# Cluster similarities of an attention kernel: the token tile becomes the stationary operand, the centroids move

## The chip, the cores and the metric

The kernel runs on one core of a Trainium2 chip. Its engines are TensorE (PE, its weight loads PEld), VectorE (DVE), ScalarE (ACT), GpSimd (POOL) and SyncE (SP), which only issues DMAs here. Each takes its instructions in its own order and waits for the others by semaphores. The metric is the device time of one execution in microseconds, median of the runs; lower is better.

## The reference, cut to what matters

Attention over 2 x 8 heads of 768 tokens and 64 dimensions, in which a token attends only to tokens of its own cluster; two dense layers follow (token count 1536, model width 512).

```python
q_n = q / (np.linalg.norm(q, axis=-1, keepdims=True) + 1e-06)      # k_n, c_n alike
q_assign = np.argmax(np.einsum('bhsd,hcd->bhsc', q_n, c_n), axis=-1)   # 16 centroids a head
k_assign = np.argmax(np.einsum('bhsd,hcd->bhsc', k_n, c_n), axis=-1)
mask = q_assign[:, :, :, None] == k_assign[:, :, None, :]
scores = np.where(mask, scale * np.matmul(q, k.transpose(0, 1, 3, 2)), -1000000000.0)
attn = softmax(scores)            # max subtracted, 1e-9 added to the sum
out = np.matmul(attn, v)
# then: h = (x @ w1) * (x @ w2) @ w3 @ w_out; out = softplus(h @ w_in) @ w_out2
```

The part at hand is the two `einsum` lines: for each token of q and of k its product with the 16 centroids of its head.

## The kernel before, in words

Work goes by pairs of heads (8 pairs). For each pair there is a *preparation* and then 12 *slots* of attention, six a head. The instructions of each engine stand in the order in which the program writes them: a loop over slots calls, for each slot, what two tables (`PE` and `EV`, for pairs 2 to 7) or (`PE1` and `EV1`, for pair 1) name for it; pair 0 is prepared by straight code ahead of the loop. A table's key is a slot relative to 12 times the pair's number, so pair 3's entry -11 is done in slot 25. Within a slot the order is: product for the row minimum (`mx_pe`, L629) and its minimum on VectorE (L638), the preparation steps, four score matmuls (`st_pe`, L659) with an exponential on ScalarE (L666), the products with v (`av_pe`, L674), and, woven in, steps of a product of two weight matrices (L520, L539).

Preparation of a pair before the change:

- `t1_pe`/`t1_ev`: q and k of one head lie side by side (64 + 64) and are transposed on TensorE, then written as two float32r tiles of 128 x 768 whose sum is the exact value: `H` (ScalarE, L318) and `L` (VectorE, L319). Rows 0 to 63 are q (scaled by -1/8), rows 64 to 127 are k.
- `centroid_turn` (once): the normalised centroids of all heads, transposed, are written into `cst`, one 128 x 128 tile a head: for the q rows and the k rows a high and a low part in columns of their own, the rest zero.
- `sims_pe` (L371): the head's `cst` tile is stationary, `H` and then `L` move, both heads of the pair summed into one PSUM bank, in two groups of tokens (512 and 256 columns): 8 matmuls. The outcome has centroids on partitions and tokens in columns.
- `sims_ev` (L61, ScalarE): the two groups are copied to `sT` in SBUF.
- `simsT_pe` (L391): for each of six chunks of 128 tokens `sT` is stationary and a 128 x 64 matrix `halves` moves. This turns tokens to partitions and adds high and low part.
- `assign` (VectorE, L404 to L418): times the reciprocal norm, maximum over 16 centroids, first hit, one-hot. `back_pe` (L428) and `back_ev` (L440) turn the one-hot rows back, and DMAs (L446) bring them into the q and k tiles of the scores.

The norms come on another way (GpSimd or ScalarE squares, VectorE sums, ScalarE roots, L282 and L283) and are first needed by `assign`. Three PSUM banks (`rb`) go round between all these steps by `take` and `give`. After the 96 slots come the dense layers (L848, L870, L1073, L1142), bound by matmuls alone.

Of the kernel before, what the change touches and what calls it, by code (L numbers as in the profile page):

```python
# [8 lines left out]
F32 = mybir.dt.float32  # L9
F32R = mybir.dt.float32r  # L10
# [3 lines left out]
ALU = mybir.AluOpType  # L14
# [4 lines left out]
P = 128  # L19
# [3 lines left out]
def f32(ap):  # L23
    return ap.bitcast(F32)
# [3 lines left out]
def fused_kernel(ctx: ExitStack, tc, q, k, v, centroids, w1, w2, w3, wo, w_in, w_o2, out):  # L28
# [6 lines left out]
    nc = tc.nc  # L35
    B, H, S, D = q.shape
# [94 lines left out]
    nc.vector.memset(bigcol[:64], BIG)  # L131
    nc.vector.memset(bigcol[64:], 1.0)

    halves = cpool.tile([P, 4, NCL], F32, name="halves")
    iv = identF.rearrange("p (g t b) -> p g t b", t=2, b=NCL)
    nc.vector.tensor_tensor(out=halves, in0=iv[:, :, 0], in1=iv[:, :, 1], op=ALU.add)
    qkcol = cpool.tile([P, 1], F32, name="qkcol")
    nc.vector.memset(qkcol[:64], -0.125)
    nc.vector.memset(qkcol[64:], 1.0)
# [40 lines left out]
    apT = pool(es_prep, "apT", bufs=4)  # L180


    cst = ap1.tile([P, H, P], F32R, name="cst")
    nc.gpsimd.memset(f32(cst), 0.0)
    oh = ap1.tile([P, QC, P], BF16, name="oh")
    nc.gpsimd.memset(oh, 0.0)
# [45 lines left out]
    def centroid_turn():  # L232
        cn = PR["cn"]
        m = take()
        nc.tensor.transpose(m[:, :P], cn.rearrange("p t d -> p (t d)"), identF)

        for ni, sc in enumerate((-8.0, 1.0)):
            rows = slice(64 * ni, 64 * ni + 64)
            mv = m[rows, :P].rearrange("p (g j c) -> p g j c", j=2, c=NCL)
            cv = cst[rows].rearrange("p (g j) x -> p g j x", j=2)  # L240
            for j in range(2):
                o = 64 * ni + 32 * j
                hi, lo = cv[:, :, j, o : o + NCL], cv[:, :, j, o + NCL : o + 2 * NCL]
                nc.vector.tensor_scalar(
                    out=hi, in0=mv[:, :, j, :], scalar1=sc, scalar2=None, op0=ALU.mult
                )
                nc.vector.scalar_tensor_tensor(
                    out=lo, in0=mv[:, :, j, :], scalar=sc, in1=f32(hi),
                    op0=ALU.mult, op1=ALU.subtract,
                )  # L250
        give(m)

    def norm_sq(pi, j):
# [103 lines left out]
        nc.gpsimd.tensor_copy(KT[0][D : D + 32, 0, :], a[D : D + 32])  # L357
        nc.gpsimd.tensor_copy(QT[0][D : D + 32, 0, :], l[:32])

    SG = ((0, 512), (512, S))  # L360

    def sims_pe(pi, g):
        if g == 0:
            PR["sT"] = ring.tile([P, S], F32, tag="w3k", name=f"sT{pi}")
        h0 = (2 * pi) % H
        m = take()
        c0, c1 = SG[g]
        n = 0
        for j in range(2):
            for t in (PR["H", j], PR["L", j]):  # L370
                nc.tensor.matmul(  # L371
                    m[:, : c1 - c0], cst[:, h0 + j, :], t[:, c0:c1],
                    start=(n == 0), stop=(n == 3),
                )
                n += 1
        PR["sm", g] = m

    def sims_ev(pi, g):
        c0, c1 = SG[g]
        act_copy(PR["sT"][:, c0:c1], PR["sm", g][:, : c1 - c0])  # L380
        give(PR["sm", g])

    NG = 4
    NA = NG * QC

    NS = NA * NCL

    def simsT_pe(pi):
        PR["sx"] = take()
        for c in range(QC):  # L390
            nc.tensor.matmul(  # L391
                PR["sx"][:, c * NG * NCL : (c + 1) * NG * NCL],
                PR["sT"][:, c * P : (c + 1) * P], halves.rearrange("p g b -> p (g b)"),
                start=True, stop=True,
            )

    def assign(pi, i):

# [188 lines left out]
    def load_v(pi):  # L587
# [10 lines left out]


    PE = {  # L600
        -16: [(t1_pe, 0)], -15: [(t1_pe, 1)], -14: [(t1_pe, 2)], -13: [(t1_pe, 3)], -11: [(sims_pe, 0)],
        -10: [(sims_pe, 1)], -9: [(simsT_pe,)], -5: [(back_pe,)],
    }
    EV = {
        -24: [(load_qk,)], -20: [(norm_sq, 0)], -19: [(norm_fold, 0)],
        -18: [(norm_sq, 1), (norm_sum, 0)], -17: [(norm_fold, 1)],
        -16: [(t1_ev, 0)], -15: [(t1_ev, 1), (norm_sum, 1), (norm_root,)],
        -14: [(t1_ev, 2), (norm_rec, 0)], -13: [(t1_ev, 3), (norm_rec, 1)], -11: [(sims_ev, 0), (norm_rec, 2)],
        -10: [(sims_ev, 1)], -8: [(assign, 0), (t_dma, 0)], -7: [(assign, 1)],
        -5: [(back_ev,)], -4: [(m_dma, 0), (t_dma, 1), (m_dma, 1)], 1: [(load_v,)],  # L610
    }

# [126 lines left out]
    class Feed:  # L739
# [39 lines left out]
        def take(self, n=1):  # L779
            now = [self.fly.pop(0) for _ in range(min(n, len(self.fly)))]  # L780
            tiles = []
            for t, (pl, store, key) in now:
                hi, lo = (
                    pl().tile([P, 512], F32R, tag="w", name=f"w{x}{key[0]}_{key[1]}") for x in "hl"
                )
                tiles.append((hi, lo))
                store[key] = (hi, lo)
            apart = decp is not None
            ds = decode([
                (t, decp.tile([P, 512], F32, tag="dec", name=f"d{k[0]}_{k[1]}") if apart else None)  # L790
                for t, (_, _, k) in now
            ])
            if apart:
                self.load(len(now))
            for (hi, lo), d in zip(tiles, ds):
                act_copy(hi, d)
                pool_sub(lo, d, f32(hi))
            if not apart:
                self.load(len(now))
# [86 lines left out]
    def steps(tab, s):  # L886
# [5 lines left out]


    PE1 = {
        0: [(t1_pe, 0)], 1: [(t1_pe, 1)], 2: [(t1_pe, 2)], 3: [(t1_pe, 3)], 4: [(sims_pe, 0)],
        5: [(sims_pe, 1)], 6: [(simsT_pe,)], 9: [(back_pe,)],
    }
    EV1 = {
        0: [(t1_ev, 0), (norm_sq, 0)], 1: [(t1_ev, 1), (norm_sum, 0)], 2: [(t1_ev, 2), (norm_sq, 1), (t_dma, 0)],
        3: [(t1_ev, 3), (norm_sum, 1), (norm_root,)], 4: [(sims_ev, 0), (norm_rec, 0), (norm_rec, 1)],  # L900
        5: [(sims_ev, 1), (norm_rec, 2), (t_dma, 1)], 7: [(assign, 0)], 8: [(assign, 1)],
        9: [(back_ev,)], 10: [(m_dma, 0), (m_dma, 1)],
    }

# [6 lines left out]
    with tc.manual_schedule():  # L911
        act_dma = nc.scalar.dma_start
        load_qk(0, [0])
        centroid_load()
        load_qk(0, [1], act_dma)
        nc.scalar.preload_act_table_set("natural_log_exp_and_others")
        w_load()
        w_load()
        t1_pe(0, 0)
        t1_pe(0, 1)  # L920
        centroid_prep()
        t1_ev(0, 0)
        t1_ev(0, 1)
        t1_pe(0, 2)
        t1_pe(0, 3)
        t1_ev(0, 2)
        t1_ev(0, 3)
        centroid_turn()
        norm_sq(0, 0)
        norm_sq(0, 1)  # L930
        load_qk(1)
        t_first()
        sims_pe(0, 0)
        sims_pe(0, 1)
        sims_ev(0, 0)
        sims_ev(0, 1)
        norm_sum(0, 0)
        norm_sum(0, 1)
        simsT_pe(0)
        norm_root(0)  # L940
        for n in range(W0):
            w_step(n, WALL[:1])
        norm_rec(0, 0)
        norm_rec(0, 1)
        norm_rec(0, 2)
        t_dma(0, 1)
        t_dma(0, 0)
        assign(0, 0)
        assign(0, 1)
        back_pe(0)  # L950
        back_ev(0)
        m_dma(0, 1, act_dma)
        w_load()
        load_v(0)
        for n in range(W0):
            w_step(n, WALL[1:])
        for s in range(NSLOT + ML + AL):
            j = s - ML
            a = j - AL
            if s < NSLOT:  # L960
                mx_pe(s)
                mx_red(s)
            if s and s % QC == 0 and s <= NSLOT:
                m_row(s // QC - 1)
            weights = s >= ML
            if weights:
                w_step(wk[0], "hlpqe")
            if a > 0 and a % 3 == 0:
                av_ev(a // 3 - 1)
            for tab in (PE1, EV1):  # L970
                for f, *x in tab.get(s, ()):
                    f(1, *x)
            if s == 4:
                load_qk(2)
            if s == 8:
                load_v(1)
            steps(PE, s)
            steps(EV, s)
            if 0 <= j < NSLOT:
                st_pe(j)  # L980
                st_exp(j)
            if weights:
                w_step(wk[0], "Abcds")
            if 0 <= a:
                av_pe(a)
            if weights:
                w_step(wk[0], "Tm")
                wk[0] += 1

            for g in range(NH):  # L990
                r = s - (ML + AL + QC * g + QC - 1)
                if r in (2, 4, 6):
                    r_ev(g, r // 2 - 1)
                if r == 8:
                    x_norm(2 * g)
                    x_norm(2 * g + 1)
            if wk[0] == NWSTEP:
                feed.load(3)

            if wk[0] > NWSTEP and s >= WSLOT:  # L1000
                i, k = divmod(s - WSLOT, 4)
                if i < 2:
                    feed.part(0, k)
                    if k == 3:
                        feed.take(1)
                        taken += 1
                elif i < 5:
                    feed.part(i - 2, k)
# [202 lines left out]
```

## Time and profile before

| | |
|---|---|
| device time, three runs | 849.31, 851.35, 854.03 us (median 851.35) |
| span of the profiled execution | 846.2 us |
| its own time beside the span | not listed; the runs shown lie 3.1 to 7.8 us above the span |
| TensorE busy | 798.1 us, 94% of the span, 3553 records |
| VectorE, ScalarE, GpSimd busy | 497.7, 396.5, 245.8 us |
| attention with preparation | about the first 375 us |

The span runs from the first to the last instruction of one profiled execution; the device time also has what lies around it. Busy TensorE time is modelled at the ends of matmuls, so the distance of starts says more on its pace than a duration does. A group "x12" in a view ordered by time is a run of like instructions, and its time is from the first start to the last end; in the chain that ended last a piece is the time by which it carried the end.

### The profile page before, as it was taken

The page shows a single profiled execution, that of the slowest core. Times are in us where ns is not written, and L with a number is a line of the kernel's source. Part 1 is how long each engine was busy: PE and PEld are TensorE (multiplying, and loading weights), DVE is VectorE, ACT ScalarE, POOL GpSimd, SP SyncE. Part 2 cuts the span into 40 slices and gives each one's busy share as a digit, 9 for nine tenths or more (in the row PEclk, how much of TensorE's full clock was granted, in tenths as well). Part 3 has the DMA queues.
Part 4 walks back from the last instruction along what each step waited for, and adds up shares of the span by engine and source line. Part 5 has one row for each costly group of instructions (what it writes and reads, how often), then busy time and mean ns, then how long its engine had stood idle before and what let it go on. Part 6 is the DMA issues. An engine that isn't in the chain of part 4 may idle for free.

```text
span 846.2 us, 10075 instructions
## 1 busy us (share of the span) xinstructions
PE 798.1 (94%) x3553; PEld 635.7 (75%) x3553; DVE 497.7 (59%) x826; ACT 396.5 (47%) x683; POOL 245.8 (29%) x232
## 2 busy tenths in 40 slices
PE   3589999979999998999999999999999999999997
PEld 3467777857777775778888888887877788888886
DVE  5878565576866565528532445564998644454443
ACT  3355445455443554555433245445555644454443
POOL 4145141145132121135201122321444222222220
PEclk9789999998999999999999999999999999999999
DMA  6875755655552555035311133430210100001001
GB/s 164 201 165 160 169 141 134 149 146 138 151 120 67 138 137 124 12 93 184 107 44 50 50 99 101 149 100 1 74 50 1 50 1 1 1 2 48 1 0 51
DMA packets 77491, 75.61 MB, mean 89 GB/s; under 512 B 46336, under 2 KB 62848, under 8 KB 77440
## 3 DMA queue, kind: packets, MB, share of 16 engines
q1 hardware_dynamic: 75476, 73.84, 32.7%
q10 hardware_dynamic: 1964, 1.12, 0.5%
q8 instruction: 28, 0.46, 0.2%
q14 instruction: 23, 0.19, 0.1%
HBM read 50.41 MB, written 3.24 MB: 63 GB/s over the span
## 4 chain that ended last, share of the span: by engine, by line
PE 77%; DVE 13%; DMA 3%; SPq 2%; ACT 2%; issue 2%; POOL 1%; DVEq 0%; POOLq 0%; ACTq 0%
PE avb L674 11%; PE rb L848 8%; PE sb L848 8%; PE sb L1073 6%; PE sb L659 6%; PE rb L1073 6%; PE mb L1142 6%; PE rb L539 5%; PE mb L870 4%; PE mb L629 3%; PE rb L1142 3%; PE avb L1142 3%; PE avb L870 2%; PE rb L870 2%; DVE mn L638 2%
## 5 line engine op out<-in xcount | busy, mean ns | idle before, releaser
L674 PE MATMUL avb<-E,v 128*128 128x384 f32 x384 | 143.3, 496 | 0.4 <-ACT t L61 0.4
L638 DVE TENSOR_REDUCE mn<-mb 128x1 f32<-128x768 f32 x92 | 87.7, 953 | 90.1 <-PE mb L629 89.5
L66 POOL TENSOR_TENSOR u<-u,t 128x512 f32<-128x512 f32 x47 | 66.7, 1420 | 167.3 <-DVE u L1096 167.3
L666 ACT ACTIVATE E<-sb 128x768 f32<-128x768 f32 x96 | 77.6, 808 | 74.3 <-PE sb L659 73.4
L659 PE MATMUL sb<-q,k 128*128 128x384 f32 (+1 forms) x384 | 92.7, 364 | 4.6 <-ACT E L666 4.0
L674 PEld LDWEIGHTS avb<-E,v 128*128 128x128 f32 x384 | 72.6, 194 | 28.8 <-ACT t L61 2.1
L629 PE MATMUL mb<-k,q 128*128 128x384 f32 x184 | 65.6, 438 | 11.6 <-DVE mn L638 9.1
L659 PEld LDWEIGHTS sb<-q,k 128*128 128x128 f32 (+1 forms) x384 | 67.8, 196 | 10.1 <-ACT E L666 6.8
L1073 PE MATMUL sb<-ys,wh_i 128*128 128x512 f32 x192 | 64.2, 395 | 3.5 <-ACT t L1084 2.2
L1073 PE MATMUL rb<-ys,wh_i 128*128 128x512 f32 x192 | 63.4, 392 | 0.0
L848 PE MATMUL rb<-xs,wh 128*128 128x512 f32 x192 | 61.7, 392 | 0.0
L848 PE MATMUL sb<-xs,wh 128*128 128x512 f32 x192 | 61.6, 392 | 0.0
L1086 DVE TENSOR_SCALAR u<-t 128x512 f32<-128x512 f32 x48 | 21.1, 440 | 68.1 <-ACT t L1085 68.1
L629 PEld LDWEIGHTS mb<-k,q 128*128 128x128 f32 x184 | 33.8, 196 | 30.9 <-DVE mn L638 13.2
L66 POOL TENSOR_TENSOR wl_o<-d_o,wh_o 128x512 fp32r<-128x512 f32 x16 | 21.6, 1351 | 121.3 <-ACT wh_o L61 121.3
L721 POOL TENSOR_TENSOR xT<-t,R 64x384 f32<-64x384 f32 x32 | 34.0, 1083 | 59.5 <-DMA R<-rd 59.3
L69 DVE TENSOR_TENSOR gl<-u,gh 128x512 fp32r<-128x512 f32 x48 | 39.6, 825 | 18.6 <-ACT gh L61 17.8
L1095 ACT ACTIVATE u<-u 128x512 f32<-128x512 f32 x48 | 30.4, 633 | 35.7 <-DVE t L1092 35.6
L1073 PEld LDWEIGHTS sb<-ys,wh_i 128*128 128x128 f32 x192 | 35.9, 188 | 13.6 <-ACT t L1084 3.3
L1073 PEld LDWEIGHTS rb<-ys,wh_i 128*128 128x128 f32 x192 | 36.1, 188 | 8.0
L848 PEld LDWEIGHTS rb<-xs,wh 128*128 128x128 f32 x192 | 36.1, 188 | 7.9
L848 PEld LDWEIGHTS sb<-xs,wh 128*128 128x128 f32 x192 | 36.1, 188 | 7.8
(208 smaller groups left out, 1787.1 us busy)
## 6 DMA issues: line engine op xcount, KB each, us to landing
w3r<-in_moe_w_dram SPq DMA_DIRECT2D x16, 512.0 KB
w12r<-in_moe_w_dram SPq DMA_DIRECT2D x16, 512.0 KB
wir<-in_moe_w_in_dram SPq DMA_DIRECT2D x16, 512.0 KB
wor<-in_moe_w_out_dram SPq DMA_DIRECT2D x16, 512.0 KB
q<-H SPq DMA_DIRECT2D x15, 384.0 KB
w3r<-in_moe_w_out_dram SPq DMA_DIRECT2D x8, 512.0 KB
k<-L SPq DMA_DIRECT2D x16, 192.0 KB
v<-in_v_dram SPq DMA_DIRECT2D x16, 192.0 KB
```

Source lines behind the costliest of these rows:

```text
L66: nc.gpsimd.tensor_tensor(out=o, in0=i, in1=hi, op=ALU.subtract)
L69: return nc.vector.tensor_tensor(out=o, in0=i, in1=hi, op=ALU.subtract)
L539: nc.tensor.matmul(m, a[:, ks], bb, start=(mc == 0 and x == 0), stop=(mc == NK - 1 and x == 2))
L629: nc.tensor.matmul(bank[:, hf, :HALF], QT[g][:, 0, c * P : (c + 1) * P], KT[g][:, 0, hf * HALF : (hf + 1) * HALF], start=True, stop=True,)
L638: nc.vector.tensor_reduce(out=MN[g][:, c : c + 1], in_=mx_bank(s)[:, :, :HALF], op=ALU.min, axis=AX.XY)
L659: nc.tensor.matmul(sbank[:, i, :HALF], KT[g][: P - 31 * n, n, ks], QT[g][: P - 31 * n, n, qs], start=(n == 0), stop=(n == 1),)
L666: nc.scalar.activation(E[j], sbank[:, :, :HALF], AF.Exp, scale=-1.0)
L674: nc.tensor.matmul(avbank[:, :HALF], V[g][:, 2 * kp + i, :], e[:, i, :], start=(kp == 0 and i == 0), stop=(kp == 2 and i == 1),)
L848: nc.tensor.matmul(bk[:, :BLK], a[:, sl], bb, start=(n == 0), stop=(n == 3 * CC - 1))
L870: nc.tensor.matmul(ybank[e][:, :BLK], a[:, es], bb, start=(fc == 0 and n == 0), stop=(fc == NFC - 1 and n == 2),)
L1073: nc.tensor.matmul(hbank[(bl * NF2 + fc) % 4][:, :BLK], a[:, sl], bb, start=(n == 0), stop=(n == 3 * CC - 1))
L1142: nc.tensor.matmul(ob, a[:, sl], bb, start=(fc == 0 and n == 0), stop=(fc == NF2 - 1 and n == 2),)
```

## The change

The similarities come out with tokens on partitions at once: the 128-token chunk of `H` or `L` is the stationary operand and the centroids move, 32 columns at a time (16 for q, 16 for k). For each head and chunk three products are summed in PSUM: H with the high part of the centroids, H with the low part, L with the high part. (The fourth, L with the low part, was in the sum before and is left out.) `cst` is laid out by high and low part, q and k rows, head and centroid; its high part is written by ScalarE, its low part by VectorE. `sT`, `halves`, `sims_ev`, `simsT_pe` and two uses of a PSUM bank a pair are gone. In the tables the similarities stand in slots -10 and -9, one head each, instead of -11 and -10 with the product with `halves` in -9.

```diff
--- before.py
+++ after.py
@@ -131,9 +131,6 @@
     nc.vector.memset(bigcol[:64], BIG)
     nc.vector.memset(bigcol[64:], 1.0)
 
-    halves = cpool.tile([P, 4, NCL], F32, name="halves")
-    iv = identF.rearrange("p (g t b) -> p g t b", t=2, b=NCL)
-    nc.vector.tensor_tensor(out=halves, in0=iv[:, :, 0], in1=iv[:, :, 1], op=ALU.add)
     qkcol = cpool.tile([P, 1], F32, name="qkcol")
     nc.vector.memset(qkcol[:64], -0.125)
     nc.vector.memset(qkcol[64:], 1.0)
@@ -180,7 +177,7 @@
     apT = pool(es_prep, "apT", bufs=4)
 
 
-    cst = ap1.tile([P, H, P], F32R, name="cst")
+    cst = ap1.tile([P, 2, 2, H, NCL], F32R, name="cst")
     nc.gpsimd.memset(f32(cst), 0.0)
     oh = ap1.tile([P, QC, P], BF16, name="oh")
     nc.gpsimd.memset(oh, 0.0)
@@ -236,18 +233,12 @@
 
         for ni, sc in enumerate((-8.0, 1.0)):
             rows = slice(64 * ni, 64 * ni + 64)
-            mv = m[rows, :P].rearrange("p (g j c) -> p g j c", j=2, c=NCL)
-            cv = cst[rows].rearrange("p (g j) x -> p g j x", j=2)
-            for j in range(2):
-                o = 64 * ni + 32 * j
-                hi, lo = cv[:, :, j, o : o + NCL], cv[:, :, j, o + NCL : o + 2 * NCL]
-                nc.vector.tensor_scalar(
-                    out=hi, in0=mv[:, :, j, :], scalar1=sc, scalar2=None, op0=ALU.mult
-                )
-                nc.vector.scalar_tensor_tensor(
-                    out=lo, in0=mv[:, :, j, :], scalar=sc, in1=f32(hi),
-                    op0=ALU.mult, op1=ALU.subtract,
-                )
+            mv = m[rows, :P].rearrange("p (h b) -> p h b", b=NCL)
+            hi, lo = cst[rows, 0, ni], cst[rows, 1, ni]
+            act_copy(hi, mv, scale=sc)
+            nc.vector.scalar_tensor_tensor(
+                out=lo, in0=mv, scalar=sc, in1=f32(hi), op0=ALU.mult, op1=ALU.subtract
+            )
         give(m)
 
     def norm_sq(pi, j):
@@ -357,42 +348,22 @@
         nc.gpsimd.tensor_copy(KT[0][D : D + 32, 0, :], a[D : D + 32])
         nc.gpsimd.tensor_copy(QT[0][D : D + 32, 0, :], l[:32])
 
-    SG = ((0, 512), (512, S))
-
-    def sims_pe(pi, g):
-        if g == 0:
-            PR["sT"] = ring.tile([P, S], F32, tag="w3k", name=f"sT{pi}")
-        h0 = (2 * pi) % H
-        m = take()
-        c0, c1 = SG[g]
-        n = 0
-        for j in range(2):
-            for t in (PR["H", j], PR["L", j]):
-                nc.tensor.matmul(
-                    m[:, : c1 - c0], cst[:, h0 + j, :], t[:, c0:c1],
-                    start=(n == 0), stop=(n == 3),
-                )
-                n += 1
-        PR["sm", g] = m
-
-    def sims_ev(pi, g):
-        c0, c1 = SG[g]
-        act_copy(PR["sT"][:, c0:c1], PR["sm", g][:, : c1 - c0])
-        give(PR["sm", g])
-
     NG = 4
     NA = NG * QC
 
     NS = NA * NCL
 
-    def simsT_pe(pi):
-        PR["sx"] = take()
+    def sims_pe(pi, j):
+        if j == 0:
+            PR["sx"] = take()
+        h = 2 * pi % H + j
+        sx = PR["sx"][:, :NS].rearrange("p (c n j b) -> p c j n b", n=2, j=2, b=NCL)
         for c in range(QC):
-            nc.tensor.matmul(
-                PR["sx"][:, c * NG * NCL : (c + 1) * NG * NCL],
-                PR["sT"][:, c * P : (c + 1) * P], halves.rearrange("p g b -> p (g b)"),
-                start=True, stop=True,
-            )
+            cs = slice(c * P, (c + 1) * P)
+            for i, (x, w) in enumerate((("H", 0), ("H", 1), ("L", 0))):
+                nc.tensor.matmul(
+                    sx[:, c, j], PR[x, j][:, cs], cst[:, w, :, h], start=(i == 0), stop=(i == 2)
+                )
 
     def assign(pi, i):
 
@@ -598,15 +569,15 @@
 
 
     PE = {
-        -16: [(t1_pe, 0)], -15: [(t1_pe, 1)], -14: [(t1_pe, 2)], -13: [(t1_pe, 3)], -11: [(sims_pe, 0)],
-        -10: [(sims_pe, 1)], -9: [(simsT_pe,)], -5: [(back_pe,)],
+        -16: [(t1_pe, 0)], -15: [(t1_pe, 1)], -14: [(t1_pe, 2)], -13: [(t1_pe, 3)],
+        -10: [(sims_pe, 0)], -9: [(sims_pe, 1)], -5: [(back_pe,)],
     }
     EV = {
         -24: [(load_qk,)], -20: [(norm_sq, 0)], -19: [(norm_fold, 0)],
         -18: [(norm_sq, 1), (norm_sum, 0)], -17: [(norm_fold, 1)],
         -16: [(t1_ev, 0)], -15: [(t1_ev, 1), (norm_sum, 1), (norm_root,)],
-        -14: [(t1_ev, 2), (norm_rec, 0)], -13: [(t1_ev, 3), (norm_rec, 1)], -11: [(sims_ev, 0), (norm_rec, 2)],
-        -10: [(sims_ev, 1)], -8: [(assign, 0), (t_dma, 0)], -7: [(assign, 1)],
+        -14: [(t1_ev, 2), (norm_rec, 0)], -13: [(t1_ev, 3), (norm_rec, 1)], -11: [(norm_rec, 2)],
+        -8: [(assign, 0), (t_dma, 0)], -7: [(assign, 1)],
         -5: [(back_ev,)], -4: [(m_dma, 0), (t_dma, 1), (m_dma, 1)], 1: [(load_v,)],
     }
 
@@ -892,13 +863,13 @@
 
 
     PE1 = {
-        0: [(t1_pe, 0)], 1: [(t1_pe, 1)], 2: [(t1_pe, 2)], 3: [(t1_pe, 3)], 4: [(sims_pe, 0)],
-        5: [(sims_pe, 1)], 6: [(simsT_pe,)], 9: [(back_pe,)],
+        0: [(t1_pe, 0)], 1: [(t1_pe, 1)], 2: [(t1_pe, 2)], 3: [(t1_pe, 3)],
+        5: [(sims_pe, 0)], 6: [(sims_pe, 1)], 9: [(back_pe,)],
     }
     EV1 = {
         0: [(t1_ev, 0), (norm_sq, 0)], 1: [(t1_ev, 1), (norm_sum, 0)], 2: [(t1_ev, 2), (norm_sq, 1), (t_dma, 0)],
-        3: [(t1_ev, 3), (norm_sum, 1), (norm_root,)], 4: [(sims_ev, 0), (norm_rec, 0), (norm_rec, 1)],
-        5: [(sims_ev, 1), (norm_rec, 2), (t_dma, 1)], 7: [(assign, 0)], 8: [(assign, 1)],
+        3: [(t1_ev, 3), (norm_sum, 1), (norm_root,)], 4: [(norm_rec, 0), (norm_rec, 1)],
+        5: [(norm_rec, 2), (t_dma, 1)], 7: [(assign, 0)], 8: [(assign, 1)],
         9: [(back_ev,)], 10: [(m_dma, 0), (m_dma, 1)],
     }
 
@@ -932,11 +903,8 @@
         t_first()
         sims_pe(0, 0)
         sims_pe(0, 1)
-        sims_ev(0, 0)
-        sims_ev(0, 1)
         norm_sum(0, 0)
         norm_sum(0, 1)
-        simsT_pe(0)
         norm_root(0)
         for n in range(W0):
             w_step(n, WALL[:1])
```

TensorE in slots 13 to 15, where pair 2 is prepared, before the change: `H`, `L` and `cst` as above, `sb` the scores, `avb` the products with v, `mb` the products for the row minimum, `rb` the shared banks.

```order
L371 MATMUL rb_102<-L_1_478,cst 128x512
L659 MATMUL sb<-q_212,k_213 128x384 x4
L674 MATMUL avb<-E_536,v_0_285 128x384 x2
L629 MATMUL mb<-k_335,q_334 128x384 x2
L371 MATMUL rb_100<-H_0_431,cst 128x256
L371 MATMUL rb_100<-L_0_432,cst 128x256
L371 MATMUL rb_100<-H_1_477,cst 128x256
L371 MATMUL rb_100<-L_1_478,cst 128x256
L659 MATMUL sb<-q_212,k_213 128x384 x4
L674 MATMUL avb<-E_565,v_0_285 128x384 x2
L629 MATMUL mb<-k_335,q_334 128x384 x2
L391 MATMUL rb_101<-halves,sT_553 128x64 x6
```

And TensorE after the change in slots 14 and 15, from the last chunk of the first head to the first chunk of the second:

```order
L364 MATMUL rb_99<-cst,H_0_463 128x2x16 x2
L364 MATMUL rb_99<-cst,L_0_464 128x2x16
L630 MATMUL sb<-q_206,k_207 128x384 x4
L645 MATMUL avb<-E_591,v_0_298 128x384 x2
L600 MATMUL mb<-k_348,q_347 128x384 x2
L364 MATMUL rb_99<-cst,H_1_509 128x2x16 x2
L364 MATMUL rb_99<-cst,L_1_510 128x2x16
```

What moved: the blocks of 4, 4 and 6 matmuls in three slots became two blocks of 18 in two slots, in the slots of the second block and of the `halves` product; the steps around them are the same.

ScalarE at pair 0, ahead of the loop, before the change (`q` and `k` are the tiles of the scores, `nrm` the norms):

```order
L318 ACTIVATE H_1_182<-rb_100,qkcol 128x384
L61 ACTIVATE q_212<-H_0_158 64x768
L61 ACTIVATE k_213<-H_0_158 64x768
L61 ACTIVATE sT_219<-rb_102 128x512
L61 ACTIVATE sT_219<-rb_100 128x256
L282 ACTIVATE nrm_230<-nrm_230 128x24
L283 ACTIVATE nrm_230<-nrm_230 128x24
```

And after it:

```order
L309 ACTIVATE H_1_180<-rb_98,qkcol 128x384
L63 ACTIVATE cst<-rb_99 64x128 x2
L61 ACTIVATE q_206<-H_0_156 64x768
L61 ACTIVATE k_207<-H_0_156 64x768
L273 ACTIVATE nrm_249<-nrm_249 128x24
L274 ACTIVATE nrm_249<-nrm_249 128x24
```

What moved: the two `sT` copies that stood ahead of the norms are gone, and two writes of `cst` stand ahead of the copies to `q` and `k`. On VectorE at this place eight writes of `cst` (64 elements each) became two (128 each).

## Rows read from the trace of the kernel before

**Rows 1.** The page's busy time of each engine: us, share, instructions.

```profile
PE 798.1 (94%) x3553; PEld 635.7 (75%) x3553; DVE 497.7 (59%) x826; ACT 396.5 (47%) x683; POOL 245.8 (29%) x232
```

**Rows 2.** The page's chain that ended last: share of the span by engine.

```profile
PE 77%; DVE 13%; DMA 3%; SPq 2%; ACT 2%; issue 2%; POOL 1%; DVEq 0%; POOLq 0%; ACTq 0%
```

**Rows 3.** Stretches: length, busy (count) of PE, PEld, DVE, ACT, POOL, clock, DMA.

```profile
170.00:200.00 30.00, 25.38 (x107) 18.64 (x106) 20.63 (x34) 15.62 (x29) 15.45 (x16) 0.89 0.55 140
200.00:320.00 120.00, 118.21 (x571) 92.78 (x570) 78.95 (x137) 56.95 (x95) 31.72 (x37) 1.00 0.52 127
```

**Rows 4.** The chain by time at the start: start us, us, piece.

```profile
14.07 0.22 DVE cst L247
...
15.32 2.91 PE rb L371 x8
...
18.66 0.23 ACT nrm L282
...
21.44 0.58 DVE rb L404
...
39.77 1.29 PE rb L391 x12
...
42.37 0.57 DVE rb L404
```

**Rows 5.** The same chain around pair 3's similarities, 100 to 112 us.

```profile
103.11 0.93 PE rb L371 x4
...
106.84 0.48 PE rb L371 x4
107.32 0.70 PE sb L659 x4
...
109.67 1.28 PE rb L391 x12
110.95 0.76 PE sb L659 x4
```

**Rows 6.** Groups by line, first 320 us: busy us, mean ns, idle before.

```profile
L629 PE MATMUL mb<-k,q 128*128 128x384 f32 x160 | 55.8, 430 | 8.3 <-DVE mn L638 5.7 <-ACT k L436 2.0 <-DMA k<-sg 0.6
...
L629 PEld LDWEIGHTS mb<-k,q 128*128 128x128 f32 x160 | 29.2, 196 | 23.7 <-DVE mn L638 9.2 <-issue 2.5 <-DVE w3r L493 1.2
...
L539 PEld LDWEIGHTS rb<-woh,w3th 128*128 128x128 f32 x64 | 12.1, 189 | 5.0 <-DVE w3tl L69 0.9
...
L391 PEld LDWEIGHTS rb<-halves,sT 128*128 128x128 f32 x96 | 12.0, 196 | 0.1
...
L428 PEld LDWEIGHTS <-oh 128*128 128x128 bf16 x48 | 3.1, 108 | 7.8 <-issue 6.4 <-DVE oh L418 1.4
```

**Rows 7.** TensorE in order of time, 55 to 85 us: start us, us, group.

```profile
66.06 1.45 PE L391 MATMUL rb<-halves,sT 128*128 128x64 f32 x12
...
79.17 0.51 PE L428 MATMUL rb<-identB,oh 128*128 128x128 bf16 x6
79.48 0.95 PE L659 MATMUL sb<-q,k 128*128 128x384 f32 x4
```

**Rows 8.** TensorE's waits, 55 to 320 us: total us, times, longest.

```profile
PE sb L659 <- ACT E L666: 4.0, 3, 2.8
```

**Rows 9.** Instructions in order of time, first 40 us.

```profile
18.05 1.84 PE L391 MATMUL rb<-halves,sT 128*128 128x64 f32 x12
```

**Rows 10.** Stretches of the start, columns as in rows 3.

```profile
25.00:30.00 5.00, 2.83 (x13) 2.46 (x14) 3.76 (x7) 2.68 (x3) 0.00 (x0) 0.50 0.58 172
...
40.00:45.00 5.00, 2.49 (x17) 1.75 (x16) 4.70 (x9) 0.65 (x2) 1.66 (x3) 1.00 1.07 217
```

**Rows 11.** Instructions in order of time around 188 us; idle before in brackets.

```profile
188.64 0.58 ACT L318 ACTIVATE H<-rb,qkcol 128x384 fp32r<-128x384 f32 x1 [3.77 <-DMA k<-H]
...
189.97 1.65 PE L659 MATMUL sb<-q,k 128*128 128x384 f32 x4 [2.82 <-ACT E L666]
```

## The prediction

> **What bounds the kernel.** I read the shares by engine first, then the chain that ended last, then the stages, then the few microseconds around one pair's similarities. TensorE is busy 798.1 of 846.2 us [rows 1], and 77% of the chain that ended last is TensorE, 2% ScalarE [rows 2]. From 200 to 320 us TensorE works 118.21 of 120 us, ScalarE 56.95 [rows 3]. So in most of the attention stage anything that lengthens TensorE's own stream lengthens the kernel, and anything taken off ScalarE does not shorten it. Two stretches differ. Between 170 and 200 us TensorE stands idle 4.6 us (25.38 of 30 busy) [rows 3]; and the start runs along the preparation of the first two pairs, through VectorE and ScalarE too [rows 4].
>
> The change touches eight pairs of heads. Pairs 2 to 7 are prepared inside the attention stage, at places where TensorE is the bound; pairs 0 and 1 at the start.
>
> **What goes out of TensorE's stream.** For one pair of the full stream (pair 3) the chain holds three blocks: four matmuls of 512 columns, 0.93 us; four of 256, 0.48 us; and the product with `halves`, 12 records, 1.28 us [rows 5]. Together 2.69 us a pair. The six matmuls with `halves` appear as twelve records; both their operands are plain float32.
>
> **What comes in.** Now 36 matmuls a pair: two heads, six chunks of 128 tokens, three terms, each with a 128x128 stationary tile and 32 moving columns. No matmul of this kind is in the trace, so I bound it.
> - The nearest row is the product with `halves`: a 128x128 stationary tile and few moving columns (64). Its records follow each other at 1.28 / 12 = 0.107 us [rows 5], although one load alone takes 196 ns [rows 6]: loads overlap matmuls and each other, and the load sets the pace. A float32r load is as long as a float32 load, 189 against 196 ns [rows 6]. So 36 x 0.107 = 3.85 us.
> - The narrowest float32r row is the 256-column one: 0.48 / 4 = 0.120 us a matmul [rows 5], so 36 x 0.120 = 4.32 us.
> - The row below is the bfloat16 transpose: six loads and six matmuls of 128 columns stand between 79.17 and 79.48 us, 0.052 us for a load and its matmul [rows 7], so 36 x 0.052 = 1.87 us.
> - The end above is the way of the `halves` product: if a narrow matmul made two records like it, 72 x 0.107 = 7.70 us.
>
> I take 0.107, the row with nearly the same shape. H is moved against by two centroid tiles in turn, so one stationary tile serves two matmuls; L629 is such a place too, and has 160 loads for 160 matmuls [rows 6], so no load is saved.
>
> At 0.107 a pair costs 3.85 - 2.69 = 1.16 us more. Six pairs: +7.0 us. The score matmuls behind the load-paced block take 0.76 us instead of 0.70 [rows 5]; there are now two such blocks a pair instead of one, about +0.05 x 6 = +0.3 us.
>
> The trace has bfloat16 loads at 108 ns on the mean against 189 for float32r [rows 6]: the quick kind of load is not given to float32r here. The Trainium skill (TensorE: Matmul & The Clock Gate, section "Weight-path perf modes — Fast Weight Load (FWL) and DoubleRow") grants the fast load to 128 weights whose type is not FP32, and by its wording float32r could have it. By the trace the six pairs cost +7.0 us, by that rule they would gain; the durations side with the trace, and the rule is kept as the fast rival below.
>
> **What is removed elsewhere.** Two ScalarE copies a pair (`sT`) go. In the stream no piece of the chain between 100 and 112 us was theirs: TensorE's blocks stood one behind the other [rows 5]. They are worth nothing there. The bank for the similarities is held a slot longer, and two other uses of a bank vanish; of TensorE's six listed waits between 55 and 320 us the largest, 4.0 us in three times, is for ScalarE's exponential and not for a bank of the preparation [rows 8], so I set this at nothing, up to 1 us either way. The smaller fill of `cst` and the missing `halves` addition lie ahead of the first data: nothing. The ring that held `sT` now turns over three tiles a pair instead of four; each is read long before its place is written again: nothing.
>
> **Pair 1.** Its second block stands where the `halves` product stood: from 39.77 us, 1.29 us, then score matmuls, a minimum on VectorE, then the assignment from 42.37 us [rows 4]. Eighteen loads instead of twelve: 6 x 0.107 = +0.64 us on that path. The first block falls into a gap of TensorE before the slot's minimum is done: nothing.
>
> **Pair 0.** Before: centroid writes on VectorE up to 15.3 us, the eight similarity matmuls from 15.32 us for 2.91 us, ScalarE's copies, then the norms (from 18.66 us on ScalarE), and the assignment at 21.44 us [rows 4]. Eight writes of 64 elements at 0.22 us each become two ScalarE copies and two VectorE subtractions of 128; I estimate each at 0.3 us, so TensorE starts about 1 us earlier, at 14.3. The norms no longer queue behind `sT`: another 1 us, so they end near 19.4. Then the similarities are late next. TensorE runs at half pace here: the eight matmuls take 2.91 us against 0.93 + 0.48 in the stream [rows 4, 5]. At half pace 36 loads need 36 x 0.213 = 7.7 us, to 22.0. Before, the twelve `halves` records from 18.05 us span 1.84 us against 1.45 in the stream [rows 9, 7]: 0.39 / 0.107, about four of them, were still slow, so the pace doubled near 18.9 us, 3.6 us after TensorE began. If it does so again, 17 loads at 0.213 and 19 at 0.107 end near 20.0. So the assignment starts 1.4 us earlier to 0.6 us later. The DMA engines are full soon after (share 1.07 from 40 to 45 us [rows 10]) and can swallow a gain. I take -0.4 us.
>
> **Sum.** 7.0 + 0.3 + 0.64 - 0.4 = +7.5 us. On the profiled span that is 846.2 + 7.5 = 853.7 us. The three runs shown have their median at 851.35 us, 5.15 above that span; the same distance gives 858.9, and I predict 859.
>
> **Rivals.**
> 1. *Cheaper loads, or the stall gives it back: no difference.* With H loaded once for its two products a pair has 24 x 0.107 = 2.57 us, -0.1. Or ScalarE's freed time moves the stall at 188 us: there `H` waits 3.77 us for a DMA, the next scores 2.82 us for ScalarE's exponential, and their block takes 1.65 us [rows 11] instead of 0.95 [rows 7]; with the slow blocks behind it some 5 us. For it: this long wait occurs in one pair only, so the order of things decides it. Against: the chain behind it starts from TensorE's scores and moves along. About 851 to 854 us.
> 2. *Loads at the bfloat16 pace: faster.* 1.87 - 2.69 = -0.82 a pair, -4.9 for six; pair 1 gains 1.29 - 18 x 0.052 = 0.35, pair 0 some 1: 851.35 - 6.3 = 845 us. It decides from below 2.69 / 36 = 0.075 us a matmul. For it: a bfloat16 load with its matmul needs 0.052 [rows 7]. Against: 189 ns loads of float32r [rows 6].
> 3. *Narrow matmuls make two records: much slower.* 7.70 - 2.69 = +5.0 a pair, +30 for six, +4.5 at the start: 886 us. For it: `halves` does so. Against: its operands are plain float32.
> 4. *The clock falls in the load-paced blocks.* A block streams 18 x 32 columns in 1.93 us. The trace has a stretch at 0.50 of the full clock after idle time [rows 10]; in the `halves` blocks of the stream the pace held [rows 5]. If both blocks ran at half pace: +3.85 a pair beside the rest, 23 more, 882 us.
>
> That the change does not do what it says I exclude: the order of instructions shows the 36 matmuls and no `sT`.
>
> **Chances.** Forecast (+4.5 to +11 us) 0.62; rival 1 0.19; rival 2 0.08; rivals 3 and 4 0.11 together. About 0.5% (4.3 us) is what a measurement of this kernel tells from no change. Faster 0.10 (rival 2 and the lucky end of rival 1), same 0.19, slower 0.71. The likeliest case alone spans 856 to 862 us (0.107 to 0.120 a load, the start's two ends). The range reaches down over most of rival 1 and up by the stall's 5 us: 850 to 867; rivals 2, 3 and 4 lie outside.
>
> **What would show it.** In the changed profile: 288 narrow matmuls with as many loads, starting 0.107 us apart, in blocks of 1.9 us at two places a pair; 128 more TensorE records; the attention stage about 7 us longer, and the stages behind it unchanged in length. Wrong would be: starts at 0.05 or 0.08 us; two records a matmul; a granted clock under 1.00 in slots with similarities; or a stall at 188 us that is gone or doubled.

## The result, and the profile after

On the chip of the prediction the kernel before took 851.97 us (median of four runs, 849.31 to 854.03) and the changed one 859.86 us (four runs, 859.05 to 860.81). The ratio is 1.0111, 95% interval 1.0074 to 1.0148: slower by 1.1%. The forecast was 859 us. (The ratio is formed over the runs and not from the two medians; the medians alone give 0.9%.)

The page of the changed kernel, parts 1 and 4, answers to [rows 1, 2]; then the new matmuls and their loads, all from one line (count; shortest, median and longest in ns; first and last start in us; form).

```profile
PE 814.5 (95%) x3681; PEld 653.1 (76%) x3681; DVE 495.7 (58%) x819; ACT 389.8 (45%) x669; POOL 244.8 (29%) x232
...
PE 78%; DVE 13%; issue 2%; ACT 2%; DMA 2%; SPq 1%; POOL 1%; ACTq 0%; DVEq 0%; POOLq 0%
```

```profile
L364 PEld LDWEIGHTS rb<-cst,H x192: 186/192/338, 14.7 to 310.2; 128*128 128x128 f32 x192
L364 PE MATMUL rb<-cst,H x192: 177/263/396, 14.7 to 310.2; 128*128 128x32 f32 x192
L364 PEld LDWEIGHTS rb<-cst,L x96: 190/192/334, 15.2 to 310.3; 128*128 128x128 f32 x96
L364 PE MATMUL rb<-cst,L x96: 262/263/375, 15.2 to 310.4; 128*128 128x32 f32 x96
```

TensorE is busy 16.4 us longer and has 3681 - 3553 = 128 records more; 192 + 96 = 288 narrow matmuls stand in the trace, one record each, and each has a load of its own (192 ns at the median). ScalarE is busy 6.7 us less, and the chain that ended last has not become shorter by it.

The chain around pair 3, start and length in us, answers to [rows 5].

```profile
111.11 1.91 PE rb L364 x18
113.03 0.79 PE sb L630 x4
...
115.47 1.92 PE rb L364 x18
117.39 0.80 PE sb L630 x4
```

Two blocks of 18 loads, 0.106 us a load, 3.83 us a pair in place of 2.69; both blocks delay the score matmuls behind them, which take 0.80 us (0.70 elsewhere).

For the length of the whole stretch of pairs 2 to 7 I take two marks in both chains: the first score maxima behind the start (slot 12), and the score block after pair 7's similarities. Before, then after:

```profile
57.04 0.58 PE mb L629 x2
...
301.76 0.70 PE sb L659 x4
```

```profile
61.28 0.58 PE mb L600 x2
...
313.07 0.70 PE sb L630 x4
```

The first mark is 4.24 us late, the second 11.31 us: 7.07 us for six pairs, 1.18 a pair. From 200 to 320 us TensorE is busy 118.04 of 120 us, as before (118.21 [rows 3]). Behind the second mark lie 545.5 us, 544.4 before.

The start is where the surprise lies. The chain at the start, answering to [rows 4]:

```profile
14.69 7.99 PE rb L364 x36
22.68 0.02 issue
22.70 0.58 DVE rb L375
...
37.90 3.23 PE rb L364 x18
41.13 0.83 PE mb L600 x2
41.96 0.21 PE rb L616
42.17 3.65 PE rb L364 x18
...
47.64 0.48 DVE rb L375
```

Pair 0's 36 loads need 7.99 us, 0.222 a load, from first to last; its assignment starts at 22.70 us (21.44 before). Pair 1's blocks take 3.23 and 3.65 us, and its assignment starts at 47.64 us, 5.27 us late: the second block begins 2.40 us later (42.17 against 39.77), takes 2.36 us more (3.65 against 1.29), and 0.51 us more lie behind it. Of this 4.24 us are left at the mark of slot 12. The windows of that stretch (length, then busy us and count of PE, PEld, DVE, ACT, POOL; granted clock, DMA share, GB/s):

```profile
30.00:38.00 8.00, 6.24 (x27) 4.98 (x25) 6.86 (x10) 3.69 (x7) 0.00 (x0) 1.00 0.61 150
38.00:40.00 2.00, 2.00 (x13) 2.00 (x12) 1.97 (x5) 0.44 (x2) 0.00 (x0) 0.56 1.03 178
40.00:46.00 6.00, 6.00 (x28) 5.80 (x28) 2.67 (x4) 0.27 (x1) 1.20 (x3) 0.50 0.88 188
```

From 40 to 46 us TensorE is busy all the time and is granted 0.50, that is 1.2 GHz; before, its window from 40 to 45 us had 1.00 [rows 10]. And in order of time, start and group:

```profile
37.87 0.26 PE L364 MATMUL rb<-cst,L 128*128 128x32 f32 x1
37.98 0.37 PE L364 MATMUL rb<-cst,H 128*128 128x32 f32 x2
38.21 0.36 PE L364 MATMUL rb<-cst,L 128*128 128x32 f32 x1
38.41 0.59 PE L364 MATMUL rb<-cst,H 128*128 128x32 f32 x2
38.84 0.37 PE L364 MATMUL rb<-cst,L 128*128 128x32 f32 x1
```

Pair 1's first block begins at the pace of the stream (three matmuls from 37.87 to 38.21, 0.11 us each) and from about 38.2 us runs at half of it (two from 38.41 to 38.84, 0.21 us each). That the block caused this fall is not shown: from 30 to 38 us TensorE had stood idle for 1.76 of 8 us, and in two later profiles with the same start (the changed kernel on another chip, then the kernel below with only its start changed) the clock fell ahead of the block, in a stretch where TensorE was busy half of the time:

```profile
34.00:37.80 3.80, 1.80 (x9) 1.25 (x6) 3.80 (x6) 0.86 (x2) 0.00 (x0) 0.87 1.02 262
```

```profile
34.00:37.80 3.80, 1.90 (x7) 1.32 (x6) 3.80 (x6) 0.59 (x2) 0.00 (x0) 0.72 0.96 260
```

What all three show is that the clock stayed at 0.50 while the blocks ran, with TensorE busy all the time (in these two, 3.70 of 3.70 us at 0.50 from 37.8 to 41.5 us).

One caution on sizes. The profiled spans differ by 858.6 - 846.2 = 12.4 us, the medians by 7.9. The changed kernel's profiled execution took 860.39 us, 1.8 over its span; by the same distance the execution before, with its span of 846.2, took about 848.0, below all its four timed runs. By this estimate it was a short one. Its first mark shows it too: in three other profiles with the start of before (two runs of the first mixed kernel below, and the kernel with the cheap part alone) that mark stands at 58.49, 59.34 and 58.79 us, in place of 57.04, so part of the 4.24 us is the short execution. Where I give prices below, they come from runs timed on one chip.

### The profile page after: what moved, and what is told of

It is laid out like the page before. It is cut to its first block, busy times and chain, and to the rows that moved or that the text cites. A ratio compares the mean times of both kernels' runs of the same rounds, so it can differ in the third digit from the quotient of the medians.

```text
span 858.6 us, 10285 instructions
## 1 busy us (share of the span) xinstructions
PE 814.5 (95%) x3681; PEld 653.1 (76%) x3681; DVE 495.7 (58%) x819; ACT 389.8 (45%) x669; POOL 244.8 (29%) x232
## 4 chain that ended last, share of the span: by engine, by line
PE 78%; DVE 13%; issue 2%; ACT 2%; DMA 2%; SPq 1%; POOL 1%; ACTq 0%; DVEq 0%; POOLq 0%
PE avb L645 12%; PE rb L819 8%; PE sb L819 8%; PE sb L630 6%; PE sb L1041 6%; PE mb L1110 5%; PE rb L1041 5%; PE rb L510 5%; PE rb L364 4%; PE mb L841 4%; PE mb L600 3%; PE rb L1110 3%; PE avb L1110 3%; PE avb L841 2%; PE rb L841 2%
```

## The experiments

Theory A: the time went to two places, the six pairs in the stream (36 loads of 0.107 us) and the start, where the load-paced blocks run at half pace. Theory B: the start's delay is swallowed later and the stream alone is the loss. They were told apart by doing one half of the change at a time. In the diffs "-" is the changed kernel and "+" the experiment, where nothing else is said.

**Old way for pairs 0 and 1.** Both ways are in the kernel; a condition picks the pairs, and GpSimd copies the centroids into the other layout. The diff is against the kernel before and shows two places of it.

```diff
+    NEW = lambda pi: pi >= 2
...
+    def simsN_pe(pi, j):
+        if not NEW(pi):
+            return
```

> Pairs 0 and 1 by the way of before (sT and halves), pairs 2 to 7 by the way of after; the second layout of the centroids is written by GpSimd in slots 6 and 7. Theory A (two costs: about 1.2 us a pair for the six pairs in the stream, and about 4.2 us at the start, where the load-paced blocks hold TensorE at half pace): the assignment of pair 0 is back at 21.4 us, the first row product of head 2 at 57 us, and the time about 4.2 us under after, near 855.5 us. Theory B (only the count of loads matters, the start is chance): no more than 0.7 us under after, 859 us.

Measured: 857.73 us against 847.47 before on that chip, ratio 1.0106 (1.0076 to 1.0136). By that ratio the stream part alone costs 0.0106 x 847.47 = 9.0 us (10.3 by the medians). Some of it belongs to the mixed kernel itself: four GpSimd copies stand in its chain at 46 us with 0.78 us, and its time lies 2.1 us above its span, in place of 1.8.

**Old way for pairs 2 to 7.** "-" is here the mixed kernel above, and one line is shown; the centroids are now written in the new layout first and copied to the old one.

```diff
-    NEW = lambda pi: pi >= 2
+    NEW = lambda pi: pi < 2
```

> The mirror image: pairs 0 and 1 by the way of after, pairs 2 to 7 by the way of before. Theory A: both blocks of the start at half pace again (pair 0 about 8 us, pair 1 above 3 us a block), the first row product of head 2 near 61 us, and the rest as before: about 4.2 us above before, 856 us. Theory B: 0.6 us above before, 852.6 us. Together with the other mixed kernel the two costs should add up to the whole difference.

Measured: 850.73 us, ratio 1.0025 (1.0005 to 1.0045): 2.1 us for the start alone, 0.4 to 3.8 by the interval. The chain of its profile has "7.90 PE rb L411 x36" for pair 0, and two blocks of 3.65 us for pair 1. So a loss at the start arrives at the end, though with less than the 4.24 us of the two profiles above. Theory A's size (4.2 us) lies just outside the interval and theory B's (0.6 us) inside it, so this run alone does not decide. To price the start once more from the other side, the change and the kernel with the old start were run beside each other on a second chip.

> The changed kernel itself, so that it stands on one chip beside the mixed kernel that follows. If the start's 4.2 us of the profile reach the end (theory A), it is 3 to 4.5 us slower than the mixed kernel with the old start (857.7 against 847.5 for before when that was measured), so 1.4% over before. If they are given back later or the mixed kernel's start was no better (theory B), it is within 1 us of it, 1.0 to 1.1% over before.

> The same kernel as the first mixed one (pairs 0 and 1 by the old way, pairs 2 to 7 by the new), once more beside after on one chip. Theory A: 3 to 4.5 us under after. Theory B: within 1 us of after.

Measured there: the changed kernel 861.17 us, ratio 1.0131 (1.0103 to 1.016) to 848.63 before; with the old start 856.56 us, ratio 1.0076 (1.0048 to 1.0103). By the ratios the whole change costs 11.1 us there, the stream part 0.0076 x 848.63 = 6.4 us, and the start the 4.7 us between the two (4.6 by their medians; no run of the one reaches into the range of the other: 859.53 to 862.47 against 854.82 to 858.5 us). Theory B, at most 1 us, falls. On the first of these chips the two halves, 9.0 and 2.1, add up to the same 11.1. So the start costs 2 to 5 us and the stream 6 to 9, and the seven of the two profiles lie between. The marks of the other profiles agree: the first stands at 57.04 to 59.34 us in four profiles with the old start and at 61.28 to 62.59 in three with the new one, 3.5 us apart on the mean, and the stretch from it to the second mark is 242.3 to 244.7 us in three profiles with the old stream and 250.0 to 252.4 in four with the new one, 7.8 us apart.

**H against the low part left out: 24 loads a pair.**

```diff
-            for i, (x, w) in enumerate((("H", 0), ("H", 1), ("L", 0))):
+            for i, (x, w) in enumerate((("H", 0), ("L", 0))):
```

> After without the product of H with the low part of the centroids (that part of the similarities is left out): 24 loads and matmuls a pair instead of 36, all else the same. If the load sets the pace: a block of 12 takes 1.28 us in the stream (0.107 a load), 7.7 us less for six pairs, and at the start 2.6 us less for pair 0 (12 loads at 0.213) and some 2 us for pair 1: 847.5 to 850 us, at or under before. If a block costs a fixed time or the moving columns set the price, no more than 12 x 0.013 = 0.2 us a pair: 858 us.

Measured: 848.89 us, ratio 1.0007 (0.9987 to 1.0027). The blocks of the stream fell in proportion, as the chain around pair 2 shows:

```profile
63.05 1.24 PE rb L364 x12
64.29 0.81 PE sb L630 x4
...
66.75 1.25 PE rb L364 x12
67.99 0.80 PE sb L630 x4
```

12 x 0.104 us. The count of loads, each with its matmul, is the price. 32 moving columns here or 64 in the float32 `halves` product make no difference in the pace (0.104 to 0.107 us). Whether the load sets it or a fixed time of each matmul is not shown, since every matmul here has a load of its own. Even a third fewer loads than the change needs only bring the kernel back to where it was.

**TensorE kept at work ahead of pair 0's similarities.** Thirteen bfloat16 matmuls of 512 columns, whose outcome nobody uses, at three places before them; one place is shown.

```diff
         centroid_turn()
+        warm(5)
         norm_sq(0, 0)
```

> After with 13 wide bfloat16 matmuls (512 columns, into a bank nobody uses yet) in TensorE's gaps between 7.7 and 14.6 us, so that it comes to pair 0's similarities at full pace. Theory A1 (the load-paced matmuls do not keep the full pace up): the first loads start 0.107 us apart, then the pace halves within the block as it did in pair 1 at 38.2 us; the block takes 5 to 6.5 us instead of 8.0 and the assignment starts at 20 to 21.2 us instead of 22.7; 1.5 to 2.5 us less in all. Theory A2 (the pace stays as it was found): the block takes 3.9 us, the assignment waits for the norms and starts near 19.7 us, 3 us less.

Measured: 857.85 us, ratio 1.0107 (1.0076 to 1.0137), and pair 0's block 5.67 us in place of 7.99. TensorE in order of time, then the windows of its two parts:

```profile
14.25 0.26 PE L368 MATMUL rb<-cst,L 128*128 128x32 f32 x1
14.36 0.37 PE L368 MATMUL rb<-cst,H 128*128 128x32 f32 x2
14.59 0.26 PE L368 MATMUL rb<-cst,L 128*128 128x32 f32 x1
...
16.41 0.59 PE L368 MATMUL rb<-cst,H 128*128 128x32 f32 x2
16.84 0.37 PE L368 MATMUL rb<-cst,L 128*128 128x32 f32 x1
17.05 0.59 PE L368 MATMUL rb<-cst,H 128*128 128x32 f32 x2
```

```profile
14.20:16.40 2.20, 2.20 (x20) 2.20 (x21) 1.89 (x3) 1.47 (x3) 0.00 (x0) 0.99 1.06 241
16.40:19.80 3.40, 3.37 (x17) 3.27 (x16) 1.40 (x3) 1.32 (x3) 2.44 (x6) 0.50 1.07 220
```

The block begins at full pace, 0.11 us a load, and at 16.4 us, with TensorE busy without a gap, the granted clock falls from 0.99 to 0.50 and the starts go to 0.21 us. The DMA engines are as full at the one pace as at the other (share 1.06 and 1.07), so they do not make the difference. The assignment starts at 19.81 us, in place of 22.70. Pair 0's block did not raise the clock in any run (24 of these matmuls took 5.31 us there, 48 in the next experiment 10.55, at half pace throughout), and here it doesn't hold it. Whether 1.5 to 2.5 us arrive at the end can't be said: the changed kernel was not timed on this chip, and its ratios on two others were 1.0111 and 1.0131; the mark of slot 12 stands at 59.36 us (61.28 and 62.59 in the changed kernel).

**All four products: 48 loads a pair.** It asks whether the price stays linear, and whether the clock also falls in the stream (rival 4).

```diff
-            for i, (x, w) in enumerate((("H", 0), ("H", 1), ("L", 0))):
+            for i, (x, w) in enumerate((("H", 0), ("H", 1), ("L", 0), ("L", 1))):
```

> After with the fourth product (L with the low part of the centroids) put back: 48 loads a pair instead of 36. If the load sets the pace: 24 x 0.107 = 2.57 us a block instead of 1.92, 1.28 us a pair more, 7.7 us for six pairs, and at the start 2.6 us for pair 0 and up to 2.6 for pair 1: 8 to 12 us over after. If a block has a fixed price: no change.

Measured: 884.27 us, ratio 1.04 (1.0372 to 1.0428), 23.1 us over the changed kernel on that chip. The expected size is missed by a factor of two. The blocks themselves are as foretold; look at what stands behind the second one. The chain, then the windows:

```profile
77.94 2.58 PE rb L364 x24
80.53 0.83 PE sb L630 x4
81.36 2.56 PE avb L645 x4
83.92 0.65 PE mb L600 x2
```

```profile
75.50:78.00 2.50, 2.50 (x13) 1.97 (x12) 0.02 (x1) 0.81 (x1) 1.50 (x2) 1.00 0.87 246
78.00:80.60 2.60, 2.60 (x24) 2.60 (x24) 1.61 (x4) 0.00 (x0) 0.70 (x1) 1.00 0.18 72
80.60:83.00 2.40, 2.40 (x7) 1.56 (x7) 0.00 (x0) 1.36 (x2) 0.00 (x0) 0.62 0.00 0
83.00:86.00 3.00, 3.00 (x11) 2.36 (x10) 1.41 (x2) 1.07 (x2) 0.00 (x0) 0.74 0.01 3
```

The second block of 24 runs at 1.00; then the clock falls, and the wide matmuls pay: 2.56 us for a block of four that takes 1.29 at 1.00. Behind the first block, from 75.5 us, it stays at 1.00. So it is in most pairs: in the 3 us behind a block the clock is 0.56 to 0.68 for five of the six second blocks and one of the six first ones, and 1.00 for the rest. In the pair without a fall (its blocks start at 274.39 and 282.20 us) twelve matmuls of 512 columns stand between the two blocks. In the changed kernel it is 1.00 behind all twelve blocks of 18. From 70 to 330 us the granted clock is 0.96 on the mean against 0.99 in the changed kernel, so about 0.03 x 260 = 8 us; the 72 further loads of the six pairs are 72 x 0.107 = 7.7 us, and the mark of slot 12 is 4.9 us later than in the changed kernel beside it (67.52 against 62.59). That makes 20.6 of 23.1.

**The same 48 loads in four blocks of 12.** This tells how the loads are placed from how many there are. "-" is here the kernel with 48 loads, which ran again beside it.

```diff
-        -10: [(sims_pe, 0)], -9: [(sims_pe, 1)], -5: [(back_pe,)],
+        -12: [(sims_pe, 0, (0, 1, 2))], -11: [(sims_pe, 0, (3, 4, 5))],
+        -10: [(sims_pe, 1, (0, 1, 2))], -9: [(sims_pe, 1, (3, 4, 5))], -5: [(back_pe,)],
```

> The kernel with 48 loads a pair (L x low put back), and for pairs 2 to 7 its matmuls stand in four blocks of 12 in four slots instead of two blocks of 24 in two; the number of loads is the same, the start (pairs 0 and 1) is unchanged. Theory C (the length of one load-paced block decides whether the clock falls behind it): blocks of about 1.28 us, and the windows behind them in the stream stay at a granted clock of 1.00; two more block boundaries a pair cost 0.1 us each, so 884.3 - 8 (clock) + 1.2 = 877 us, ratio 1.034 to the kernel before. Theory D (the share of load-paced work over a longer stretch of the stream decides, or the 8 us come from something else than the clock): the falls to 0.5 to 0.8 stay, 883 to 887 us, ratio 1.04 or more. A third possibility: the bank of the similarities is held two slots longer and TensorE waits for a bank, several us per pair, to be seen in the waits of t1 or of back, 890 us and more.

> The kernel with 48 loads a pair as run earlier, on this chip as the control of the kernel with four blocks of 12: all theories 882 to 886 us, ratio 1.037 to 1.043, granted clock down to 0.6 to 0.8 behind the blocks of 24 in the stream.

Measured: 875.47 us, ratio 1.0318 (1.0288 to 1.0348); the control 883.83 us, ratio 1.0414 (1.0376 to 1.0451). 8.4 us come back with the same loads. The clock can account for it: its mean over an execution is 0.980 in the five timed runs and 0.971 in the six of the control, by estimate 0.009 x 880 = 8 us. The windows from 65 to 100 us, pair 2 and the slots behind it, of the four blocks and of the control:

```profile
65.00:100.00 35.00, 32.59 (x175) 25.44 (x173) 24.20 (x44) 17.68 (x30) 14.32 (x14) 1.00 0.53 136
```

```profile
65.00:100.00 35.00, 32.45 (x156) 24.90 (x155) 21.82 (x38) 16.24 (x28) 14.33 (x14) 0.90 0.45 116
```

So not the number of loads but their placing decides, and the size is theory C's. That it is the length of one block is not shown: the four blocks also stand in twice as many slots, 3.7 us from start to start, so how close the loads stand changed as well; and the first blocks of 24, mostly without a fall behind them, speak against the length of one block alone. The four blocks keep one slow stretch, 0.77 from 200 to 230 us: it begins behind the wait of 2.79 us for the exponential that ends at 208.45 us, and the first block of 12 behind it, at 213.16 us, runs at half pace.

**The cheap part of the change alone.** The kernel before, with the high part of the centroids written by ScalarE and the norms of pair 0 ahead of the copies. "-" is the kernel before.

```diff
-                nc.vector.tensor_scalar(
-                    out=hi, in0=mv[:, :, j, :], scalar1=sc, scalar2=None, op0=ALU.mult
-                )
+                act_copy(hi, mv[:, :, j, :], scale=sc)
...
-        sims_ev(0, 0)
-        sims_ev(0, 1)
         norm_sum(0, 0)
         norm_sum(0, 1)
-        simsT_pe(0)
         norm_root(0)
+        sims_ev(0, 0)
+        sims_ev(0, 1)
+        simsT_pe(0)
```

> Before with one thing taken from after: the high part of the centroids is written by ScalarE, and pair 0's norms stand ahead of the sT copies on ScalarE; all similarities by the old way. The assignment of pair 0 starts near 19.8 us instead of 21.4. If the start is a chain that reaches the end: 1 to 1.6 us under before. If the DMAs of the start swallow it: no difference.

Measured: 849.79 us, ratio 1.001 (0.9989 to 1.0031): no difference, the gain expected isn't there. The chain of its profile shows where it stopped:

```profile
18.70 2.83 PE rb L389 x12
21.55 0.58 DVE rb L402
```

The norms are done sooner, but the product with `halves` now follows behind the copies and ends at 21.5 us, still at half pace for most of its length (1.84 us before [rows 9]); pair 0's assignment starts at 21.55 us, not earlier than 21.44. No version in these runs beats the kernel before.

## Why the prediction was right, and which step was wrong

- **The six pairs in the stream: right.** Foretold +7.0 and +0.3 for the boundaries, found 7.07 between the marks of the two profiles, and 6.4 and 9.0 us by the timed kernels with the old start. The choice that carried it was the pace of the `halves` product, 0.107 us, over the narrow float32r row (0.120) and the bfloat16 row (0.052); found 0.106 to 0.107. The boundary term was too small: 0.10 us at two blocks a pair is 0.20, against 0.06 at one before, so 0.14 x 6 = 0.8 us in place of 0.3.
- **No load saved, one record a matmul: right.** 288 loads for 288 matmuls, so rival 1 by cheaper loads and rival 3 fall, and rival 2 by loads of 192 ns. The rule of the Trainium skill (TensorE: Matmul & The Clock Gate, section "Weight-path perf modes — Fast Weight Load (FWL) and DoubleRow"), by whose wording float32r could have the fast load, does not show here: a float32r load takes 192 ns at the median, as a float32 one does (196 on the mean [rows 6]).
- **ScalarE's copies worth nothing in the stream: right.** The wait for the exponential stays TensorE's largest. The waits from 55 to 330 us (total us, times, longest), answering to [rows 8]:

```profile
PE sb L630 <- ACT E L637: 3.6, 3, 2.5
```

- **Rival 1 by the stall: no.** That row is 4.0 us in the kernel before, and from 170 to 200 us TensorE is busy 25.72 us (25.38 [rows 3]): neither gone nor doubled.
- **Pair 0: wrong.** The step was "if it does so again": that the pace doubles 3.6 us after TensorE begins. Before, those 3.6 us were eight matmuls of 512 and 256 columns and the first `halves` records; in the changed kernel they are load-paced matmuls of 32 columns, and the pace doubled at no time in 7.99 us. I took the time of the rise from the row and left out what TensorE was doing ahead of it. The norms did end earlier, as said, and the similarities were late next; -0.4 us became +1.26 us at the assignment. Even the later end of the estimate, the whole block at half pace and 0.6 us later, was short by 0.7 us: the block began at 14.69 us and not at 14.3, and took 7.99 us and not 7.7.
- **Pair 1: wrong.** +0.64 us assumed the stream's pace, and the first block was said to fall into a gap. At half pace the two blocks take 6.88 us, the first one reaches past its gap, and the assignment comes 5.27 us later. A granted clock under 1.00 in slots with similarities was named as a sign of being wrong; it came true here, and not in the stream.
- **Rival 4 was mis-sized by place.** I gave it one price, the whole stream at half pace. Half pace in load-paced blocks exists, but at the start; in the stream the clock stayed at 1.00 in and behind all twelve blocks of 18, and only with blocks of 24 did it fall, behind half of them.
- **The number 859 owes something to a second error.** The start's two terms were 4 us too low at the mark of slot 12. The distance of 5.15 us from span to median was too large: 1.8 us is what lies around the span, and the remaining 3.3 us were the short execution that was profiled. The two nearly cancel: 846.2 + 12.4 + 1.8 = 860.4 us. They are not quite independent, since the short execution also has the early mark at 57.04 us; but that they cancel is luck, and no part of the working foresaw it.

What stays open: whether the start is worth nearer 2.1 us (0.4 to 3.8, with the old stream) or 4.7 (with the new one; the marks say 3.5); what lowers the clock ahead of pair 1's first block; whether the length of a block or how close the blocks stand lowers it in the stream; and the 2.5 us of the kernel with 48 loads that its parts leave over.

## What to carry to other kernels

To swap the stationary and the moving operand is to trade columns for loads: count the loads, take their pace from the trace's narrowest matmul of the same type, and compare with the columns saved; a removed copy on an engine that isn't waited for pays for nothing. Narrow matmuls that run at the pace of their loads belong between wide ones and in small blocks with room between them; in a stretch with little wide work, as at the start of a kernel, price them at half the clock. And look at the distance of the profiled span to its own run before using a median.

## What the runs showed of the hardware that was not expected

- A TensorE that is busy without a gap can lose its clock, and can fail to get it back: with the early matmuls it was busy 2.20 of 2.20 us at 0.99 and then fell to 0.50 within the same block, and in the changed kernel it was busy 6.00 of 6.00 us at 0.50 (40 to 46 us), most of it load-paced matmuls of 32 columns. In the stream all twelve blocks of 18 loads left it at 1.00; of twelve blocks of 24, six were followed by 0.56 to 0.68, mostly the second of a pair, 5 to 7 us behind the first.
- Ahead of the first fall the granted clock does not tell the pace. In the changed kernel pair 0's window reads 1.00 at 0.222 us a load, twice the stream's time:

```profile
14.70:20.00 5.30, 5.30 (x25) 5.26 (x25) 3.65 (x7) 3.20 (x6) 1.80 (x5) 1.00 1.07 222
```

At the start go by the distance of starts.
